# Twelve units of work between seven products: two lots of six in place of three of four

## The chip, the core and the metric

The program runs on one core of a Trainium2 chip. Its time is the device time of one execution in microseconds. The kernel is a chain of an attention layer and two feed-forward layers, all in float32 accuracy; TensorE (PE in the rows) does the products, VectorE (DVE), ScalarE (ACT) and GpSimd (POOL) read results out and prepare operands, and SyncE (SP) issues the transfers.

## The reference

Shapes: q, k, v are 4 x 8 x 576 x 64 (batch, heads, sequence, head size); w_in of both layers is 512 x 2048 and w_out 2048 x 512; there are 2304 tokens.

```python
scores = np.where(mask, scale * q @ kT + bias, -1e9)      # window of 128 keys, slopes per head
attn = softmax(scores) @ v                                # 2304 x 512 after the heads are joined
h = attn @ moe_w_in;  r = np.maximum(h, 0);  x = (r * r) @ moe_w_out
h = x @ moe2_w_in;    sp = np.log1p(np.exp(h));  out = (h * np.tanh(sp)) @ moe2_w_out
```

The change lies in the last line, the second layer: a product with w_in, the function h * tanh(softplus(h)), called Mish, and a second product with w_out.

## The kernel before, in words

Every float32 operand is split into a high part and a low part, and a product is the sum of three matmuls: high by high, high by low, low by high. Attention and the first layer fill the first 500 us.

The second layer takes its 2304 tokens in three superblocks of 768 and walks through 24 groups, eight per superblock (the loop `for g in range(24)`). In a group the first product is made by Strassen's scheme (in Winograd's form): seven products of half blocks instead of eight. Each is a call of `product` (matmuls in line 1174): six pairs of a weight load and a matmul, of which the rows show six matmuls of 128 x 384, into one bank of PSUM. In groups 1 to 8 the products use two banks in turn (`turns["p"] % 2`), so product n+2 may start when the result of product n has been read out.

Seven products give four results, c11, c22, c12 and c21, which the read-outs put together: product 1 is copied by ScalarE (line 1731); VectorE reads the others with a sum or a difference (lines 1734, 1738, 1742, 1745 and 1747, 1751, 1756 for products 2 to 7). Behind each of the four results ScalarE applies Mish twice (`mish`, lines 1197 and 1198), and VectorE makes the low part g from the two (`mish_low`, line 1203), which `done()` calls behind the next read-out.

In the first superblock (groups 0 to 7) the second product is a plain one. Its work for a group is 12 units (`o_chunk`, lines 1217 to 1219: three matmuls of 128 x 512 into one of six accumulators, acc 0 to 5), and they are run in the group that follows, groups 1 to 8, in the gaps between its seven products. The list `share` says how many units are run behind each product. Units 1 to 6 work on c11 and c22 of the group before, units 7 to 12 on c12 and c21.

The rest of the loop body is done behind the units of the same gap, in groups 1 to 7: `ring2_load` brings and splits the rows of w_out (casts in line 1155 on ScalarE, low parts in line 1159 on VectorE), `t_prepare` makes sums of them for the later superblocks, which use Strassen's scheme in the second product too (two differences on VectorE, line 1254, behind product 4 and two behind product 6; two casts in line 1259 on ScalarE behind product 7), and `t_lows` makes their low parts (line 1265, behind product 2 of the next group). In groups 4 to 7 `run_jobs` also prepares the input of the next superblock in steps, one behind each of products 2, 4, 5, 6 and 7: subtractions on GpSimd (line 1091), casts on ScalarE (line 1096) and low parts on VectorE (line 1100). Every engine works through its instructions in the order in which the program issues them.

Of the kernel before, what the change touches and what calls it, by code (L numbers as in the profile page):

```python
# [33 lines left out]
def two_layers(  # L34
# [541 lines left out]
    def m_out(l, j, fc, part):  # L576
        n = size[j]
        if fc == 0 and part == 0:
            per = 512 // n
            t = [  # L580
                ps_o.tile([P, 512], F32, tag=f"o{e}", name=f"o{l}_{j}_{e}")
                for e in range(KC // per)
            ]
            ops_[l, j] = [t[e // per][:, e % per * n :] for e in range(KC)] if per > 1 else t
        wh, wl = whl[l, ways[j][fc]]
        g = gs[l, j, fc]
        first, last = fc == 0, fc == FC - 1


        per, r = 512 // n, slice(0, n)  # L590
        for e in range(KC):
            o, ws = ops_[l, j][e][:, r], slice(DM + e * P, DM + (e + 1) * P)
            if part == 0:
                start = first and e % per == 0
                nc.tensor.matmul(o, wh[:, ws], g[:, 0, r], start=start, stop=False)  # L595
                nc.tensor.matmul(o, wl[:, ws], g[:, 0, r], start=False, stop=False)  # L596
            else:
                stop = last and e % per == per - 1
                nc.tensor.matmul(o, wh[:, ws], g[:, 1, r], start=False, stop=stop)  # L599
        if part == 1:  # L600
            gs.pop((l, j, fc))
# [50 lines left out]
    def relu2_b(a):  # L652
        g, gg, n = a
        nc.vector.tensor_tensor(  # L654
            g[:, 1, 0:n], gg[:, 0:n], g[:, 0, 0:n].bitcast(F32), op=ALU.subtract
        )
# [487 lines left out]
    def ring2_load(g, k):  # L1144
        if k == 0:
            for e in range(2):
                t = raw2[e] = ap["c"].tile([P, DM], F32R, tag="c", name=f"v{g}_{e}", bufs=4)
                nc.sync.dma_start(out=t.bitcast(F32), in_=w2d[2 * g + e])
        elif k == 3:
            for e in range(2):  # L1150
                n = 2 * (g % 2) + e
                ring2[g, e] = [
                    xp.tile([P, 512], F32R, tag=f"x{hl}{n}", name=f"v{hl}{g}_{e}") for hl in "hl"
                ]
                nc.scalar.copy(ring2[g, e][0], raw2[e].bitcast(F32))
        elif k == 4:
            for e in range(2):
                hi, lo = ring2[g, e]
                nc.vector.tensor_tensor(
                    lo, raw2[e].bitcast(F32), hi.bitcast(F32), op=ALU.subtract  # L1160
                )
# [39 lines left out]
    def mish_low(a):  # L1201
        t, u = a
        nc.vector.tensor_tensor(t[:, 1, :], u, t[:, 0, :].bitcast(F32), op=ALU.subtract)
# [3 lines left out]
    def o_chunk(s, g, t, f, h, c):  # L1207

        first, last = g % 8 == 0 and f == h, g % 8 == 7 and f != h
        k = 3 * h + c  # L1210
        if g % 8 == 0 and (s, k) not in acc:
            acc[s, k] = (ps_o if k < 4 else ps_b).tile(
                [P, 512], F32, tag=f"o{k}", name=f"acc{s}_{k}"
            )
        o, (wh, wl) = acc[s, k], ring2[g, f]
        hi, lo = (t[:, z, c * P : (c + 1) * P] for z in range(2))
        nc.tensor.matmul(o, hi, wh, start=first, stop=False)  # L1217
        nc.tensor.matmul(o, hi, wl, start=False, stop=False)  # L1218
        nc.tensor.matmul(o, lo, wh, start=False, stop=last)  # L1219
# [64 lines left out]
    def block_tile(s, b, pair_):  # L1284
        k = 4 * pair_ + b
        name = f"a{s}_{b}_{pair_}"
        if k < 14:
            return ap["x"].tile([P, 2, TH], F32, tag=f"x{k}", name=name)
        if k == 14:
            return ap["x"].tile([P, 2, TH], F32, tag="g1", name=name)  # L1290
        return gp.tile([P, 2, 512], F32, tag="g", name=name, bufs=2)[:, :, 0:TH]
# [385 lines left out]
    for g in range(24):  # L1677
        s, m = divmod(g, 8)
        units_ = []
        if g == 0:  # L1680
            relu2_b(pend)
            ring2_load(0, 4)
            units_ = [lambda: m_out(*prev, 0), lambda: m_out(*prev, 1)]
            share = [1, 1, 0, 0, 0, 0, 0]
        elif g < 9:
            for k, (f, h) in enumerate(((0, 0), (1, 1), (0, 1), (1, 0))):
                for c in (2, 0, 1) if k == 3 else range(3):
                    t = todo[k]
                    units_.append(
                        lambda t=t, f=f, h=h, c=c, s=(g - 1) // 8, g=g - 1: o_chunk(s, g, t, f, h, c)  # L1690
                    )
            share = [0, 4, 0, 4, 0, 4, 0]
        else:
            share = [0] * 7
        todo, lows = [], []

        def done():
            while lows:
                mish_low(lows.pop(0))

        def made_of(u, name):
            if s:
                a, e = blocks2[s, BLK[name[1:3]], m // 2], m % 2
                nc.scalar.activation(a[:, e, :], u, AF.Mish)  # L1704
                return
            a = mish(u, name)
            todo.append(a[0])
            lows.append(a)

        if s and m % 2 == 0:  # L1710
            for b in range(4):
                blocks2[s, b, m // 2] = block_tile(s, b, m // 2)
        sub, add = ALU.subtract, ALU.add
        tt = nc.vector.tensor_tensor
        for k, (a, x) in enumerate(
            (
                ("a11", "b11"),
                ("a12", "b21"),
                ("s2", "t2"),
                ("s3", "t3"),  # L1720
                ("s1", "t1"),
                ("s4", "b22"),
                ("a22", "t4"),
            )
        ):
            if g == 16:
                run_jobs(1)
            ps = product(g, s, k, a, x)
            if k == 0:
                p1 = u_tile(f"p1_{g}")  # L1730
                nc.scalar.copy(p1, ps)
            elif k == 1:
                u = u_tile(f"c11_{g}")
                tt(u, ps, p1, op=add)
                made_of(u, f"g11_{g}")
            elif k == 2:
                u2 = u_tile(f"u2_{g}")
                tt(u2, ps, p1, op=add)
                done()
            elif k == 3:  # L1740
                u3 = u_tile(f"u3_{g}")
                tt(u3, ps, u2, op=add)
            elif k == 4:
                u = u_tile(f"c22_{g}")
                tt(u, ps, u3, op=add)  # L1745
                u4 = u_tile(f"u4_{g}")
                tt(u4, ps, u2, op=add)
                made_of(u, f"g22_{g}")
            elif k == 5:
                u = u_tile(f"c12_{g}")  # L1750
                tt(u, ps, u4, op=add)
                done()
                made_of(u, f"g12_{g}")
            else:
                u = u_tile(f"c21_{g}")
                tt(u, u3, ps, op=sub)
                done()
                made_of(u, f"g21_{g}")
            for _ in range(share[k]):
                units_.pop(0)()  # L1760
            if g == 0 and k == 2:
                m_evac(0, NB - 1)
            if (g, k) in ((8, 6), (9, 1), (9, 3)):
                o_evac(0, {6: 2, 1: 0, 3: 1}[k])
            if 4 <= g < 8 and k in (1, 3, 4, 5, 6):
                run_jobs(1)
            if 0 < g < 9 and k == 1:
                t_lows(g - 1)
            if 0 < g < 8:
                ring2_load(g, k)  # L1770
                t_prepare(g, k)
            if g == 16 and k == 3:
                flush()
            if s and m and k == 0:
                sums3(s, m - 1)
            if s and m in (3, 4, 5, 6) and k in (1, 4):
                t_load(s, 2 * (m - 3) + (k == 4))
            if s and m == 7 and 2 <= k < 6:
                low2(s, k - 2)
            if s and m == 7 and 1 <= k < 5:  # L1780
                high2(s, k - 1)
            if g + 2 < 24 and g not in (14, 15) and k in (1, 4, 5, 6):
                ring1_load((g + 2) % 8, g + 2, ("ra", "rc", "rd", "rb")[max(k - 3, 0)])
            if 0 < g < 10 and k == (5 if g == 9 else 2):
                store_later()
        done()
        if g == 0:
            jobs += x_prepare(1)
        if s and m == 7:
            products2(s)  # L1790
# [85 lines left out]
```

## Time and profile before

| | us |
|---|---|
| time, median of 3 runs | 865.79 (865.5 to 866.45) |
| the profiled execution | 866.81 |
| its span, first to last instruction | 864.9 |
| TensorE busy (matmuls) | 857.0 (99%) |
| VectorE busy | 624.5 (72%) |
| ScalarE busy | 498.8 (58%) |
| GpSimd busy | 249.4 (29%) |

Groups 1 to 8, with which the change deals, lie between 509 and 634 us. A matmul's rows overlap, since the engine starts one before the one ahead has left it; the distance between two starts is what a matmul costs, and a row of x6 is a whole product. VectorE's rows overlap a little in the same way. "Idle before, releaser" in brackets is the time in which the engine stood still before the row, and what ended it.

### The profile page before, as it was taken

How to read it: one execution, taken by the hardware profiler on the slowest of the kernel's cores; microseconds unless marked ns; L12 is line 12 of the kernel's file. 1: busy time of each engine (PE TensorE's matmuls, PEld its weight loads, DVE VectorE, ACT ScalarE, POOL GpSimd, SP SyncE). 2: the span in 40 equal slices, each digit the busy share in tenths (PEclk: the TensorE clock that was granted, in tenths of full speed). 3: DMA queues.
4: the chain of work that ended last, by engine and by line, in shares of the span. 5: the costliest groups of instructions: out<-in, count | busy, mean ns of one | idle time of the engine just before them, and what ended most of it. 6: DMA issues, size and time to landing. Idle time of an engine off the chain costs nothing.

```text
span 864.9 us, 14890 instructions
## 1 busy us (share of the span) xinstructions
PE 857.0 (99%) x4794; PEld 752.7 (87%) x4794; DVE 624.5 (72%) x1414; ACT 498.8 (58%) x1179; POOL 249.4 (29%) x301
## 2 busy tenths in 40 slices
PE   8999999999999999999999999999999999999998
PEld 5688889998888888888888899999899999999887
DVE  5899998646596979876767456578645688755984
ACT  6888887876565656555555464545433547234641
POOL 4411213745665646643002100022024200144000
PEclk9999999999999999999999999999999999999999
DMA  8366694853765758765666978798879598988574
GB/s 285 111 219 208 197 319 140 276 185 96 269 225 207 226 152 289 249 212 168 211 214 223 364 243 290 260 313 291 268 237 366 188 306 282 316 278 281 190 266 152
DMA packets 109757, 206.98 MB, mean 239 GB/s; under 512 B 13808, under 2 KB 49008, under 8 KB 109680
## 3 DMA queue, kind: packets, MB, share of 16 engines
q1 hardware_dynamic: 109680, 206.03, 71.4%
q8 instruction: 39, 0.64, 0.3%
q14 instruction: 38, 0.31, 0.1%
HBM read 154.60 MB, written 51.38 MB: 238 GB/s over the span
## 4 chain that ended last, share of the span: by engine, by line
PE 96%; DMA 1%; DVE 1%; SPq 0%; POOL 0%; issue 0%; ACT 0%; POOLq 0%
PE h L567 23%; PE p L1174 20%; PE m L1406 11%; PE o L595 8%; PE o L596 8%; PE o L599 8%; PE o L505 3%; PE acc L1218 3%; PE acc L1219 3%; PE acc L1217 3%; PE m L1395 2%; PE pt L429 1%; PE sc L334 1%; PE sc L333 1%; PE o L526 1%; DMA wraw<-in_w 1%
## 5 line engine op out<-in xcount | busy, mean ns | idle before, releaser
L595 PE MATMUL o<-g,wh 128*128 128x512 f32 (+1 forms) x320 | 118.5, 377 | 0.0
L596 PE MATMUL o<-g,wl 128*128 128x512 f32 (+1 forms) x320 | 115.9, 369 | 0.0
L635 ACT ACTIVATE r<-h 128x512 f32<-128x512 f32 (+1 forms) x80 | 44.3, 553 | 94.3 <-PE h L567 86.0
L567 PE MATMUL h<-xh,wh 128*128 128x512 f32 (+1 forms) x320 | 81.5, 376 | 0.0
L654 DVE TENSOR_TENSOR g<-gg,g 128x512 fp32r<-128x512 f32 (+1 forms) x80 | 59.9, 749 | 29.8 <-ACT g L649 21.7
L567 PE MATMUL h<-xl,wh 128*128 128x512 f32 (+1 forms) x320 | 79.0, 369 | 0.0
L599 PE MATMUL o<-g,wh 128*128 128x512 f32 (+1 forms) x320 | 79.0, 369 | 0.0
L1704 ACT ACTIVATE a<-c 128x384 f32<-128x384 f32 x64 | 33.7, 526 | 78.5 <-DVE c L1745 41.8
L567 PE MATMUL h<-xh,wl 128*128 128x512 f32 (+1 forms) x320 | 78.8, 368 | 0.0
L465 POOL TENSOR_SCALAR_AFFINE_SELECT pT<-p 128x128 f32<-128x128 f32 (+2 forms) x80 | 52.6, 679 | 90.7 <-ACT p L453 90.5
L595 PEld LDWEIGHTS o<-g,wh 128*128 128x128 f32 x320 | 60.3, 189 | 9.8 <-issue 0.5
L596 PEld LDWEIGHTS o<-g,wl 128*128 128x128 f32 x320 | 60.4, 189 | 9.3
L1406 PE MATMUL m<-tt,hi 128*128 128x512 f32 x280 | 66.0, 390 | 0.0
L567 PEld LDWEIGHTS h<-xl,wh 128*128 128x128 f32 x320 | 56.9, 189 | 10.4
L599 PEld LDWEIGHTS o<-g,wh 128*128 128x128 f32 x320 | 56.8, 189 | 10.3
L567 PEld LDWEIGHTS h<-xh,wl 128*128 128x128 f32 x320 | 56.9, 189 | 10.1
L261 POOL TENSOR_TENSOR ulo<-uraw,uhi 128x256 fp32r<-128x256 f32 (+1 forms) x44 | 43.6, 991 | 70.8 <-ACT uhi L258 51.0
L387 ACT ACTIVATE p<-p,st 128x128 f32<-128x128 f32 (+1 forms) x144 | 59.0, 412 | 8.4 <-DVE st L372 8.3
L1406 PEld LDWEIGHTS m<-tt,hi 128*128 128x128 f32 x280 | 51.9, 188 | 10.2
L567 PEld LDWEIGHTS h<-xh,wh 128*128 128x128 f32 x320 | 54.3, 189 | 7.3 <-ACT xh L544 0.3
L1304 POOL TENSOR_TENSOR s<-a,a 128x384 f32<-128x384 f32 x14 | 14.2, 1012 | 155.9 <-ACT a L1704 155.9
L1174 PE MATMUL p<-x_t,rc 128*128 128x384 f32 x288 | 58.2, 336 | 0.0
(162 smaller groups left out, 2045.8 us busy)
## 6 DMA issues: line engine op xcount, KB each, us to landing
wraw<-in_w SPq DMA_DIRECT2D x64, 512.0 KB, 4.5
tt<-t2d SPq DMA_DIRECT2D x112, 256.0 KB, 4.6
ra<-w1d SPq DMA_DIRECT2D x24, 512.0 KB, 5.4
rc<-w1d SPq DMA_DIRECT2D x24, 512.0 KB, 4.5
rd<-w1d SPq DMA_DIRECT2D x24, 512.0 KB, 5.1
uraw<-in_qkT SPq DMA_DIRECT2D x24, 320.0 KB, 4.6
uraw<-in_qkT SPq DMA_DIRECT2D x24, 256.0 KB, 5.1
wh<-wsd SPq DMA_DIRECT2D x12, 512.0 KB, 6.4
```

Of the source, the lines that this page charges most:

```text
L261: sub(u.lo[:, 0 : u.nk], u.raw[:, 256:n], u.hi[:, 256:n].bitcast(F32), op=ALU.subtract)
L387: nc.scalar.activation(probs(i, s), probs(i, s), AF.Exp, bias=u.st[:, s : s + 1], scale=-1.0, accum_out=u.st[:, sums + s : sums + 1 + s],)
L465: nc.gpsimd.affine_select(out=u.pT[:, 0:heads, k : 2 * n : 2, :][:, :, a:], in_=p[:, 0:heads, a:n], pattern=[[0, heads * (n - a)], [0, P / ...
L567: nc.tensor.matmul(ph[:, 0:n], w[:, c * P : (c + 1) * P], xs[j, c][k][:, 0:n], start=t == 0, stop=t == len(terms) - 1,)
L595: nc.tensor.matmul(o, wh[:, ws], g[:, 0, r], start=start, stop=False)
L596: nc.tensor.matmul(o, wl[:, ws], g[:, 0, r], start=False, stop=False)
L599: nc.tensor.matmul(o, wh[:, ws], g[:, 1, r], start=False, stop=stop)
L635: nc.scalar.activation(r[:, 0:n], ph[:, 0:n], AF.Relu)
L654: nc.vector.tensor_tensor(g[:, 1, 0:n], gg[:, 0:n], g[:, 0, 0:n].bitcast(F32), op=ALU.subtract)
L1174: nc.tensor.matmul(ps, w[:, z, c * P : (c + 1) * P], t[c], start=n == 0, stop=n == 5)
L1406: nc.tensor.matmul(o[c][:, r], a, ts2[s, q][:, r], start=start, stop=stop)
L1704: nc.scalar.activation(a[:, e, :], u, AF.Mish)
```

## The change

One list of numbers is another. The seven entries are the gaps behind products 1 to 7 of a group, for groups 1 to 8.

```diff
-            share = [0, 4, 0, 4, 0, 4, 0]
+            share = [0, 6, 0, 0, 6, 0, 0]
```

Before, four units stood behind each of products 2, 4 and 6. Now six stand behind product 2 and six behind product 5. The order of VectorE's, ScalarE's, GpSimd's and SyncE's instructions is the same in both kernels; only TensorE's changes.

The first place is TensorE in group 1, from the last unit of the first lot on (`acc` are units, `p` are products 3, 4 and 5, three rows each):

```order
+L1219 MATMUL acc_5_6181<-vh_1_6013,g_0_6100 128x512
+L1174 MATMUL p_1_6189<-x_t_5759,rc_5968 128x384 x2
+L1174 MATMUL p_1_6189<-x_t_5760,rc_5968 128x384 x2
+L1174 MATMUL p_1_6189<-x_t_5759,rc_5968 128x384 x2
+L1174 MATMUL p_1_6207<-x_t_5763,rd_5970 128x384 x2
+L1174 MATMUL p_1_6207<-x_t_5764,rd_5970 128x384 x2
+L1174 MATMUL p_1_6207<-x_t_5763,rd_5970 128x384 x2
+L1174 MATMUL p_1_6226<-x_t_5767,rc_5968 128x384 x2
+L1174 MATMUL p_1_6226<-x_t_5768,rc_5968 128x384 x2
+L1174 MATMUL p_1_6226<-x_t_5767,rc_5968 128x384 x2
 L1217 MATMUL acc_3_6173<-vh_0_6010,g_0_6115 128x512
```

Product 5, which stood behind a lot, now follows product 4 directly, and the second lot follows it.

The second place is TensorE at the end of the same group, behind the last unit (products 6 and 7):

```order
 L1219 MATMUL acc_1_6165<-vh_1_6013,g_0_6130 128x512
+L1174 MATMUL p_1_6262<-x_b_5815,rd_5970 128x384 x2
+L1174 MATMUL p_1_6262<-x_b_5816,rd_5970 128x384 x2
+L1174 MATMUL p_1_6262<-x_b_5815,rd_5970 128x384 x2
 L1174 MATMUL p_1_6279<-x_t_5819,rb_5966 128x384 x2
 L1174 MATMUL p_1_6279<-x_t_5820,rb_5966 128x384 x2
```

Product 6, which stood ahead of the last lot, now stands behind it, so that products 6 and 7 and then 1 and 2 of the next group follow each other.

The third place is VectorE in group 4, from the read-out of product 6 to that of product 7, in the changed kernel:

```order
L1751 TENSOR_TENSOR c_4_6759<-p_4_6752,u_4_6718 128x384
L1203 TENSOR_TENSOR g_4_6720<-c_4_6716,g_4_6720 128x384
L1100 TENSOR_TENSOR x_b_6746<-xb_1_0_6656,x_b_6745 128x384
L1254 TENSOR_TENSOR t_4_0_6705<-v_1_6624,t_4_0_6705 128x256
L1254 TENSOR_TENSOR t_4_1_6706<-t_4_0_6705,v_1_6624 128x256
L1756 TENSOR_TENSOR c_4_6781<-u_4_6693,p_4_6774 128x384
```

Here nothing moved: before the change the same six stand in the same order, with other buffer numbers. In groups 1 to 3 the row of line 1100 isn't there, in group 8 only the first and the last are.

## Rows read from the trace of the kernel before

**Rows 1.** Page, part 4: the chain that ended last, share by engine.

```profile
PE 96%; DMA 1%; DVE 1%; SPq 0%; POOL 0%; issue 0%; ACT 0%; POOLq 0%
```

**Rows 2.** Windows of groups 3, 4: us, busy by engine, PEclk, DMA share, GB/s.

```profile
540.46:556.10 15.64, 15.64 (x80) 14.11 (x79) 9.51 (x19) 6.73 (x13) 0.00 (x0) 1.00 0.82 268
556.10:571.74 15.64, 15.64 (x80) 14.11 (x79) 11.50 (x20) 7.45 (x15) 4.42 (x4) 1.00 0.91 311
```

**Rows 3.** Waits of weight loads, 500 to 865: total us, times, longest.

```profile
PEld p L1174 <- ACT p L1731: 0.3, 1, 0.3
```

**Rows 4.** Timeline of PE, group 3: start us, us, engine, line, operation.

```profile
540.46 2.24 PE L1174 MATMUL p<-x_b,ra 128*128 128x384 f32 x12
...
542.54 0.39 PE L1217 MATMUL acc<-vh,g 128*128 128x512 f32 x1
...
545.30 1.23 PE L1174 MATMUL p<-x_t,rc 128*128 128x384 f32 x6
546.36 1.20 PE L1174 MATMUL p<-x_t,rd 128*128 128x384 f32 x6
...
555.03 1.23 PE L1174 MATMUL p<-x_t,rb 128*128 128x384 f32 x6
556.10 2.24 PE L1174 MATMUL p<-x_b,ra 128*128 128x384 f32 x12
```

**Rows 5.** Timeline of DVE and ACT, group 3 (1756 belongs to product 7 of group 2).

```profile
540.65 0.55 DVE L1756 TENSOR_TENSOR c<-u,p 128x384 f32<-128x384 f32 x1 [0.92 <-PE p L1174]
...
542.36 0.56 DVE L1203 TENSOR_TENSOR g<-c,g 128x384 fp32r<-128x384 f32 x1 [0.68 <-ACT c L1198]
...
543.26 0.47 ACT L1731 COPY p<-p 128x384 f32<-128x384 f32 x1
...
553.57 0.55 DVE L1751 TENSOR_TENSOR c<-p,u 128x384 f32<-128x384 f32 x1
...
554.04 0.55 DVE L1203 TENSOR_TENSOR g<-c,g 128x384 fp32r<-128x384 f32 x1
...
554.50 0.42 DVE L1254 TENSOR_TENSOR t<-v,t 128x256 f32<-128x256 f32 x1
...
554.96 0.42 DVE L1254 TENSOR_TENSOR t<-t,v 128x256 f32<-128x256 f32 x1
```

**Rows 6.** Timeline of DVE, groups 4 and 5: spacings of lines 1100 and 1254.

```profile
570.14 0.55 DVE L1100 TENSOR_TENSOR x_b<-xb,x_b 128x384 fp32r<-128x384 f32 x1
570.61 0.42 DVE L1254 TENSOR_TENSOR t<-v,t 128x256 f32<-128x256 f32 x1
...
579.82 0.42 DVE L1254 TENSOR_TENSOR t<-v 128x256 f32<-128x256 f32 x1
580.16 0.42 DVE L1254 TENSOR_TENSOR t<-v,v 128x256 f32<-128x256 f32 x1
...
587.17 0.43 DVE L1254 TENSOR_TENSOR t<-t,v 128x256 f32<-128x256 f32 x1
587.58 0.55 DVE L1756 TENSOR_TENSOR c<-u,p 128x384 f32<-128x384 f32 x1
```

**Rows 7.** Timeline, start of group 9: products 1 and 2, ScalarE's copy, product 4.

```profile
634.30 2.25 PE L1174 MATMUL p<-x_b,ra 128*128 128x384 f32 x12
...
635.98 0.48 ACT L1731 COPY p<-p 128x384 f32<-128x384 f32 x1
...
637.67 1.20 PE L1174 MATMUL p<-x_t,rd 128*128 128x384 f32 x6
```

**Rows 8.** Timeline of POOL and DVE, group 4.

```profile
562.59 1.01 POOL L1091 TENSOR_TENSOR t<-xb,xb 128x384 f32<-128x384 f32 x1 [82.27 <-DMA xb<-x1d]
562.68 1.34 DVE L1203 TENSOR_TENSOR g<-c,g 128x384 fp32r<-128x384 f32 x1
...
566.92 1.01 POOL L1091 TENSOR_TENSOR t<-t,xb 128x384 f32<-128x384 f32 x1
567.07 0.56 DVE L1745 TENSOR_TENSOR c<-p,u 128x384 f32<-128x384 f32 x1 [1.10 <-PE p L1174]
```

## The prediction

> **What bounds the kernel now.** The chain of waits comes first: 96% of it is TensorE [rows 1], so the question is only whether TensorE gets other work or other waits. Second, the table of windows, cut at the starts of the groups that the change touches: a group lasts 15.64 us and TensorE is busy for 15.64 of them, at a granted clock of 1.00, its full level; group 4, in which GpSimd works too, is as long as group 3 [rows 2]. There is nothing to win here but seams. Third, the list of waits of the weight loads (they run ahead of the matmuls and so meet a semaphore first): from 500 us to the end it holds one line, 0.3 us in total [rows 3]. TensorE waits for nobody behind this stage either, so what is lost here arrives at the end in full.
>
> Fourth, TensorE's own timeline in group 3 [rows 4]. I call the products of a group 1 to 7, and X the start of product 7. Products 1 and 2 take 2.08 us together (540.46 to 542.54), so 1.04 each; four units of the second product take 2.76 (542.54 to 545.30), so six take 4.14. The product behind a lot is 0.03 longer than the one behind a product (1.23 against 1.20; 555.03 to 556.10 is 1.07). Now these products alternate between two banks: product n+2 can begin only when the result of product n has been read out. Lots of units lie between most such pairs and give the reader time. The run 7, 1, 2 is the longest without a lot now.
>
> Fifth, VectorE in the same group [rows 5]. It reads product 7 (line 1756) from 540.65, 0.19 after product 1 has started, for 0.55, until 541.20; product 2 starts at 541.50. So this hand-off has 0.30 us of air, and VectorE is free when it is wanted. What it does behind product 6 is the important part: the read-out of product 6 (line 1751, 553.57), then the low part of c22 (line 1203, 554.04), then two differences for the t matrices (line 1254, 554.50 and 554.96). Before the change all this lies under four units and product 7.
>
> **The change part by part.** *The lots.* Nothing is added or taken away: 12 units per group in 8 groups before and after, and each row on VectorE, ScalarE, GpSimd and in the DMA queue keeps its place in its own queue; only TensorE's rows move. TensorE's sequence from one lot to the next was 2, 2 and 3 products long; it is now 3 (products 3, 4, 5) and 4 (6, 7, 1, 2). One lot less per group is one seam less: 8 x 0.03, so 0.2 us gained at most, and no less than nothing.
>
> *The lots' inputs and what their reading frees.* Every unit comes as early as before or earlier, and its inputs come from the group before: the last of them, the low part of c21, is done at 542.36 + 0.56 = 542.92, 1.7 us behind read-out 7 [rows 5], and the second lot, which reads it, stands behind product 5. The tiles that the units read come free earlier. No wait from here: 0.
>
> *The run 3, 4, 5.* Product 5 now needs the read-out of product 3 with only product 4 in between. That is the distance that 7, 1, 2 has now: 0.19 + 0.55 behind the next product's start, 0.30 of air [rows 4, 5]. VectorE has had a lot of 4.14 us before it to work off its queue. 0, but with little air.
>
> *The run 6, 7, 1, 2.* Three hand-offs. Product 1 needs read-out 6: VectorE is idle ahead of it, so 0.19 + 0.55 again, 0. Product 2 needs read-out 7, and that stands in VectorE's queue behind the four instructions that follow product 6. Earlier these were under four units; now product 7 ends while they run. From the rows: read-out 6 starts at X + 0.19; low of c22 0.47 later, the first difference 0.46 after that, the second 0.46 (it needs the first), and read-out 7 follows a difference by 0.34 (579.82 to 580.16) to 0.41 (587.17 to 587.58) [rows 5, 6]. So it starts at X + 1.92 to 1.99 and ends 0.55 later, at X + 2.47 to 2.54. Product 2 is due at X + 2.08. It is late by 0.39 to 0.46.
>
> What lateness costs beyond itself: in the only stall of the later trace ScalarE's copy ends at 635.98 + 0.48 = 636.46, product 3 was due at 634.30 + 2.08 = 636.38, and the product behind it starts at 637.67 and not at 637.42 [rows 7]. Late by 0.08, lost 0.25: 0.17 on top, since the weight load has to go ahead and the pipeline to fill. I take the same here: 0.56 to 0.63, middle 0.60.
>
> In groups 4 to 7 one more instruction stands in that queue, the low part of a tile for the next superblock (line 1100), 0.47 long (570.14 to 570.61) [rows 6]. There the loss is 1.03 to 1.10, middle 1.07. Both differences are made in groups 1 to 7, so it is the passages 1|2, 2|3, 3|4 at 0.60 and 4|5, 5|6, 6|7, 7|8 at 1.07: 1.80 + 4.28 = 6.08 us. In group 8 nothing stands between the two read-outs: 0.
>
> *Behind the stall.* Does it breed another? ScalarE's copy of product 1 ends 2.53 us after read-out 7 (541.20 to 543.73) [rows 5], so at about X + 5.0; product 3, which wants that bank, is due at X + 2.65 + 1.04 + 4.14 = X + 7.8. In groups 4 to 7 one more cast runs on ScalarE, the size of the copy, and the air is still over 2 us. The queue for the DMA waits for products and read-outs too, but loads for a group are issued two groups ahead, so half a microsecond is hidden by 15. Nothing.
>
> *GpSimd.* Its four subtractions in group 4 run from 562.59 to 567.93, and there the low part of a g tile took 1.34 us instead of 0.55 [rows 5, 8]. They end 11.8 us behind the start of the group (556.10); the queue behind product 6 starts 15.2 us or more behind it. I count 0. That a VectorE instruction stretches so has its rule in the Trainium skill (SBUF — State Buffer, Who interferes with whom): one with two inputs in SBUF waits out a GpSimd instruction that reads SBUF, one with at most one doesn't. The trace agrees with both halves: a read-out from PSUM that starts at 567.07, while the last subtraction runs, takes 0.56 [rows 8].
>
> *Sum.* 6.08 - 0.2 = 5.9 us. The profiled execution took 866.81 us, 1.0 more than the median of 865.79; the loss is the same for both: 872.7 there, 871.7 as a median. The ends of this case: without the 0.17 for the restart 3 x 0.43 + 4 x 0.90 - 0.2 = 4.7; with the long ends throughout 6.3 - 0. So 870.5 to 872.1.
>
> **The rivals.** *A: VectorE is in time, not slower.* The two differences need loads that are long there, so they could be done while the second lot of units runs, where VectorE has idle time; then read-out 7 is not late and one seam per group is saved: 865.6. It decides at a queue of 1.2 us from read-out 6 to read-out 7: 0.19 + 1.2 + 0.55 + 0.17 is about 2.08. Against it: the order of VectorE's rows puts both differences behind read-out 6, and in the trace each engine keeps its order; what the rows show is 1.73 or more. For it: only that the spacing of these instructions could shrink. 6%.
>
> *B: the tight hand-offs fail as well.* Products 3 to 5 and 6 to 1 have 0.30 of air, and 0.17 of it is wanted for an undisturbed start. If the air is gone, by a tenth or two of delay on VectorE, 16 hand-offs lose some 0.15 each: 2.4 more, 874.1. Against it: today's 7 to 2 has the same air and loses nothing in seven passages. 10%.
>
> *C: GpSimd's subtractions get into the queue behind product 6* in groups 4 and 6: at least one instruction stretched in each, 2 x (1.34 - 0.55) = 1.6 more, 873.3. It takes loads that land 3.4 us later than now. 3%. The page named above gives the mechanism; the price is the rows'.
>
> *D: half as much.* If the restart costs nothing on top (7 x 0.17 = 1.2 less) and all spacings in the queue but the first are 0.34, as where a difference follows one that it doesn't need (2 x 0.12 x 7 = 1.7 less), 6.08 - 2.9 - 0.2 = 3.0 are left: 868.8. Against it: 554.50 to 554.96 has the spacing of the dependent pair. 9%.
>
> **How the numbers follow.** The forecast as worked out has 72%, A 6%, B 10%, C 3%, D 9%. The likeliest is 871.7. The range takes in D's upper end, B and C: 869.0 to 874.5; outside stay A, and the ends of B and D. About 0.2%, 1.7 us, is what a measurement of this kernel can tell from no change. Faster by more would need more than all seams of the stage give (24 x 0.03 = 0.7 us): 1%. Within it: A and the smallest of D, 7%. Slower: 92%.
>
> **What would show it.** In the changed kernel's list of waits of the weight loads a line for products (1174) behind VectorE's line 1756 has to appear, seven times, six to seven microseconds in all. Cut at the starts of product 1, group 1 stays at 15.6 us, groups 2 to 4 go to about 16.2, groups 5 to 8 to about 16.7. Read-out 7 has to start without idle time right behind the second difference, 1.7 us behind read-out 6, or 2.2 in groups 4 to 7. The stage from group 9 on keeps its length. I am wrong if product 2 follows product 1 without a gap (A), if gaps stand ahead of product 5 or 1 (B), or if line 1254 or 1100 is stretched behind product 6 (C).

## The result and the profile after

The changed kernel takes 870.73 us against 865.64 before, a ratio of 1.0055 with a 95% interval of 1.0044 to 1.0067: by the ratio about 4.8 us slower (3.8 to 5.8). In a second comparison (e1_again, below) it is 871.31 against 865.59, 1.0062 (1.0048 to 1.0076), so 5.4 us (4.2 to 6.6). The forecast was 871.7, 5.9 us slower.

One of the six executions of the changed kernel, the one profiled first, ran TensorE at about half its pace from beginning to end (1716.93 us): it counts in the median of 870.73 but not in the ratio. The rows here are those of the same program in e1_again, which took 872.17 us in the profiled execution, 5.36 more than the profiled execution before.

The page of the changed kernel, part 4, the chain by engine (before: [rows 1]):

```profile
PE 94%; DVE 3%; DMA 1%; issue 1%; SPq 0%; POOL 0%; ACT 0%; POOLq 0%
```

The list of waits of the weight loads from 500 us on (us in total, times, longest; before: [rows 3]):

```profile
PEld p L1174 <- DVE c L1756: 6.2, 7, 1.1
PEld p L1174 <- ACT p L1731: 0.3, 1, 0.3
```

The first line is new: seven times a product waits for VectorE's read-out of product 7. The windows of groups 1 to 8, cut at the starts of product 1 (us, busy time by engine with the number of rows, PEclk, DMA share, GB/s; before: [rows 2]):

```profile
509.27:524.87 15.60, 15.60 (x79) 14.12 (x79) 8.87 (x18) 5.87 (x12) 0.00 (x0) 1.00 0.91 305
524.87:541.02 16.15, 15.86 (x79) 14.06 (x79) 9.41 (x20) 6.64 (x14) 0.00 (x0) 1.00 0.81 261
541.02:557.19 16.17, 15.88 (x79) 14.07 (x79) 9.42 (x20) 6.65 (x14) 0.00 (x0) 1.00 0.80 260
557.19:573.33 16.14, 15.85 (x79) 14.05 (x79) 11.35 (x20) 7.04 (x15) 4.39 (x4) 1.00 0.93 310
573.33:589.96 16.63, 15.87 (x79) 14.07 (x79) 11.76 (x25) 8.68 (x19) 0.00 (x0) 1.00 0.80 254
589.96:606.60 16.64, 15.88 (x80) 14.08 (x79) 12.21 (x22) 7.45 (x16) 4.40 (x4) 1.00 0.89 299
606.60:623.23 16.63, 15.87 (x79) 14.07 (x79) 11.76 (x25) 8.68 (x19) 0.00 (x0) 1.00 0.81 253
623.23:639.86 16.63, 15.87 (x79) 14.07 (x79) 7.83 (x16) 4.96 (x11) 0.00 (x0) 1.00 0.71 221
```

The table has the three steps of the forecast: group 1 isn't longer than before, groups 2 to 4 are at 16.15, groups 5 to 8 at 16.63. Together they last 639.86 - 509.27 = 130.59 us. Before the change they last from 509.14 (the row below) to 634.30 [rows 7], 125.16 us: 15.68 for group 1 and 15.64 for each of the others. So the stage is 5.4 us longer, and that is the whole loss: the profiled executions differ by 5.36. The granted clock is 1.00 throughout. The row of the kernel before with which group 1 starts:

```profile
509.14 2.27 PE L1174 MATMUL p<-x_b,ra 128*128 128x384 f32 x12
```

One short passage and one long one in the timeline (start us, us, engine, line, operation; before: [rows 4, 5]). First the passage from group 3 to group 4, from product 7 on:

```profile
556.15 1.20 PE L1174 MATMUL p<-x_t,rb 128*128 128x384 f32 x6
...
556.35 0.56 DVE L1751 TENSOR_TENSOR c<-p,u 128x384 f32<-128x384 f32 x1 [2.87 <-PE p L1174]
556.83 0.55 DVE L1203 TENSOR_TENSOR g<-c,g 128x384 fp32r<-128x384 f32 x1
...
557.02 1.05 PEld L1174 LDWEIGHTS p<-x_b,ra 128*128 128x128 f32 x6
557.19 1.21 PE L1174 MATMUL p<-x_b,ra 128*128 128x384 f32 x6
557.29 0.42 DVE L1254 TENSOR_TENSOR t<-v,t 128x256 f32<-128x256 f32 x1
...
557.74 0.42 DVE L1254 TENSOR_TENSOR t<-t,v 128x256 f32<-128x256 f32 x1
...
558.09 0.55 DVE L1756 TENSOR_TENSOR c<-u,p 128x384 f32<-128x384 f32 x1
...
558.68 1.00 PEld L1174 LDWEIGHTS p<-x_b,ra 128*128 128x128 f32 x6 [0.61 <-DVE c L1756]
558.69 1.31 PE L1174 MATMUL p<-x_b,ra 128*128 128x384 f32 x6 [0.29 <-DVE c L1756]
...
559.84 0.39 PE L1217 MATMUL acc<-vh,g 128*128 128x512 f32 x1
```

Product 7's row ends at 557.35, and VectorE is then in the first of its two differences. Read-out 7 starts at 558.09 without idle time, ends at 558.64, and product 2 starts 0.05 later. It was due at 557.19 + 1.04 = 558.23. Undisturbed, a product's first weight load (PEld) starts 0.17 ahead of its first matmul (557.02 and 557.19). Behind the wait both start together, and product 2 takes 1.15 to the next start (559.84) and not 1.04.

Then the passage from group 4 to group 5, which has the instruction of line 1100 in the queue as well:

```profile
572.29 1.20 PE L1174 MATMUL p<-x_t,rb 128*128 128x384 f32 x6
...
572.49 0.56 DVE L1751 TENSOR_TENSOR c<-p,u 128x384 f32<-128x384 f32 x1 [0.95 <-PE p L1174]
572.97 0.55 DVE L1203 TENSOR_TENSOR g<-c,g 128x384 fp32r<-128x384 f32 x1
...
573.33 1.21 PE L1174 MATMUL p<-x_b,ra 128*128 128x384 f32 x6
573.43 0.55 DVE L1100 TENSOR_TENSOR x_b<-xb,x_b 128x384 fp32r<-128x384 f32 x1
...
574.70 0.55 DVE L1756 TENSOR_TENSOR c<-u,p 128x384 f32<-128x384 f32 x1
...
575.30 1.33 PE L1174 MATMUL p<-x_b,ra 128*128 128x384 f32 x6 [0.76 <-DVE c L1756]
```

Read-out 7 comes 2.21 us behind read-out 6 here, and 1.74 in the short passage. "0.29" and "0.76" in brackets are less than the time lost, because a matmul's row lasts longer than the distance to the next.

### The profile page after: what moved, and what is told of

Read it like the earlier page. It is cut to its first block, busy times and chain, and to the rows that moved or that the text cites. A ratio compares the mean times of both kernels' runs of the same rounds, so it can differ in the third digit from the quotient of the medians.

```text
span 1715.2 us, 14885 instructions
## 1 busy us (share of the span) xinstructions
PE 1710.2 (100%) x4794; PEld 1257.2 (73%) x4794; DVE 606.0 (35%) x1414; ACT 502.9 (29%) x1179; POOL 230.2 (13%) x301
## 4 chain that ended last, share of the span: by engine, by line
PE 100%; POOL 0%; DVE 0%; issue 0%; POOLq 0%
PE h L567 24%; PE p L1174 21%; PE m L1406 11%; PE o L595 8%; PE o L596 8%; PE o L599 8%; PE o L505 3%; PE acc L1218 3%; PE acc L1219 3%; PE acc L1217 3%; PE m L1395 2%; PE pt L429 2%; PE sc L333 1%; PE sc L334 1%; PE o L526 1%; PE sc L310 1%
## 5 line engine op out<-in xcount | busy, mean ns | idle before, releaser
L595 PE MATMUL o<-g,wh 128*128 128x512 f32 (+1 forms) x320 | 203.7, 638 | 0.0
L596 PE MATMUL o<-g,wl 128*128 128x512 f32 (+1 forms) x320 | 199.6, 626 | 0.0
L567 PE MATMUL h<-xh,wh 128*128 128x512 f32 (+1 forms) x320 | 156.5, 642 | 0.0
L599 PE MATMUL o<-g,wh 128*128 128x512 f32 (+1 forms) x320 | 151.9, 627 | 0.0
L567 PE MATMUL h<-xl,wh 128*128 128x512 f32 (+1 forms) x320 | 150.8, 627 | 0.0
L567 PE MATMUL h<-xh,wl 128*128 128x512 f32 (+1 forms) x320 | 150.7, 632 | 0.0
L1406 PE MATMUL m<-tt,hi 128*128 128x512 f32 x280 | 133.4, 674 | 0.0
L595 PEld LDWEIGHTS o<-g,wh 128*128 128x128 f32 x320 | 97.2, 304 | 41.7 <-issue 37.8
L599 PEld LDWEIGHTS o<-g,wh 128*128 128x128 f32 x320 | 92.3, 308 | 43.7 <-issue 37.0
L1174 PE MATMUL p<-x_b,ra 128*128 128x384 f32 x288 | 105.7, 558 | 0.0
L1174 PEld LDWEIGHTS p<-x_t,rc 128*128 128x128 f32 x288 | 87.2, 304 | 15.9 <-issue 11.0
L1174 PEld LDWEIGHTS p<-x_b,ra 128*128 128x128 f32 x288 | 86.9, 305 | 14.9 <-issue 10.0
```

Source lines behind the costliest of these rows:

```text
L567: nc.tensor.matmul(ph[:, 0:n], w[:, c * P : (c + 1) * P], xs[j, c][k][:, 0:n], start=t == 0, stop=t == len(terms) - 1,)
L1174: nc.tensor.matmul(ps, w[:, z, c * P : (c + 1) * P], t[c], start=n == 0, stop=n == 5)
L1406: nc.tensor.matmul(o[c][:, r], a, ts2[s, q][:, r], start=start, stop=stop)
```

## The experiments

Two theories stood against each other. The queue theory says that the time is lost only because read-out 7 stands behind other work in VectorE's queue when products 6, 7, 1 and 2 follow each other. The order theory says that the new order of products and units costs by itself, through the tight hand-offs and the seams. Times of the kernel before in the same comparisons: 865.59 us for e1 to e4, 865.03 for e5 to e8.

**e1_again**, the changed kernel.

> The changed kernel once more, for an undisturbed trace. Queue theory (read-out 7 stands on VectorE behind the low part of c22, the two t differences and, in groups 4 to 7, the low part of line 1100): 870.6 us; seven waits of product 2 for line 1756, about 0.5 to 0.65 us each in groups 2 to 4 and 0.9 to 1.1 in groups 5 to 8; group 1 stays at 15.6. Rival, order theory (the new order of products and units costs by itself, at the tight hand-offs from product 3 to 5 and 6 to 1 and at the seams): the same time, but gaps of 0.1 to 0.3 us ahead of products 5 and 1 in all eight groups, group 1 and group 9 among them.

871.31 us, and the rows above: waits of product 2 in groups 2 to 8, none of products 5 and 1, none in group 1.

**e2_t_early**: the second pair of differences is issued behind product 5, under the second lot.

```diff
-                t_prepare(g, k)
+                t_prepare(g, {4: 5, 5: 4}.get(k, k))
```

> The changed kernel with the second pair of t differences issued behind product 5 instead of product 6, so that they lie under the second lot. Queue theory: nothing is late in passages 1|2 to 3|4; in 4|5 to 7|8 read-out 7 starts at X + 0.19 + 3 x 0.47 = 1.60 and ends at 2.15, 0.07 behind the due time, 0.07 to 0.24 lost each; the time is 865.6 - 0.2 + 0.3 to 1.0 = 865.7 to 866.4. Order theory: VectorE's queue doesn't matter, 870.6 stays.

865.7 us, ratio 0.9999 (0.9990 to 1.0009). Its waits, and the windows of a group behind a short passage (3) and behind a long one (6):

```profile
PEld p L1174 <- DVE c L1756: 1.1, 4, 0.3
```

```profile
538.94:554.51 15.57, 15.57 (x79) 14.08 (x79) 9.59 (x20) 6.81 (x14) 0.00 (x0) 1.00 0.81 270
585.91:601.74 15.83, 15.83 (x79) 14.06 (x79) 11.43 (x22) 7.37 (x16) 4.35 (x4) 1.00 0.94 315
```

Of seven waits four are left, of 0.3 us, and those are the four passages in which line 1100 still stands in the queue. Two differences in another place on VectorE give the time back, with the lots where the change put them: the order theory is gone. By the rows some 0.5 us of loss is left (four passages of 15.83 - 15.57 = 0.26, less the 0.56 that e3 below shows for fewer lots), which the ratio is too wide to show. VectorE's rows in the passage from group 4 to group 5, from read-out 6 to read-out 7:

```profile
569.25 0.56 DVE L1751 TENSOR_TENSOR c<-p,u 128x384 f32<-128x384 f32 x1 [0.43 <-PE p L1174]
...
570.66 0.55 DVE L1756 TENSOR_TENSOR c<-u,p 128x384 f32<-128x384 f32 x1
```

**e3_both_early**: as e2, and the step of line 1100 goes too. The steps are one list, worked off in order, so not this step alone moves: those that stood behind products 4, 5 and 6 now stand behind 3, 4 and 5.

```diff
-            if 4 <= g < 8 and k in (1, 3, 4, 5, 6):
+            if 4 <= g < 8 and k in (1, 2, 3, 4, 6):
```

> As e2, and in groups 4 to 7 the step for the next superblock that stood behind product 6 is issued behind product 3, so that only the low part of c22 stands between read-outs 6 and 7. Queue theory: no passage is late, one seam per group is saved, 865.4 against 865.6 before the change, which can't be told apart. Order theory: 870.6.

865.0 us, ratio 0.9991 (0.9982 to 1.0000). No wait for VectorE is left, and its groups are shorter than those before the change. Windows of groups 2 and 6, and TensorE around the first lot of group 4:

```profile
524.05:539.62 15.57, 15.57 (x79) 14.09 (x79) 9.60 (x20) 6.71 (x14) 0.00 (x0) 1.00 0.83 271
586.35:601.92 15.57, 15.57 (x79) 14.08 (x79) 11.73 (x22) 7.52 (x16) 4.28 (x4) 1.00 0.95 320
```

```profile
557.27 0.39 PE L1217 MATMUL acc<-vh,g 128*128 128x512 f32 x1
...
561.39 1.23 PE L1174 MATMUL p<-x_t,rc 128*128 128x384 f32 x6
562.46 1.20 PE L1174 MATMUL p<-x_t,rd 128*128 128x384 f32 x6
563.50 1.20 PE L1174 MATMUL p<-x_t,rc 128*128 128x384 f32 x6
```

15.57 against 15.64 [rows 2]: one lot less saves 0.07 per group, 0.5 in all. Products 3, 4 and 5 follow each other without a gap. Its groups are the shortest of all the kernels here; by its time alone it can just about not be told from the one before.

**e4_run_of_four**: the kernel before with only the run 6, 7, 1, 2.

```diff
-            share = [0, 4, 0, 4, 0, 4, 0]
+            share = [0, 4, 0, 4, 4, 0, 0]
```

> The kernel before with the last lot of four moved ahead: four units behind each of products 2, 4 and 5. The run 3, 4, 5 isn't made, the run 6, 7, 1, 2 is. Queue theory: the whole loss of the change and one seam more per group than it, 870.6 to 871.0. Order theory: one of the two new kinds of run is gone, the loss is about half, 868.

871.34 us, ratio 1.0063 (1.0049 to 1.0077). Windows of groups 3 and 6:

```profile
539.71:555.93 16.22, 15.93 (x79) 14.08 (x79) 9.51 (x20) 6.65 (x14) 0.00 (x0) 1.00 0.80 259
588.86:605.55 16.69, 15.93 (x79) 14.08 (x79) 11.52 (x22) 7.46 (x16) 4.37 (x4) 1.00 0.91 298
```

Against 15.64 this is 0.58 and 1.05 lost. The run of four alone makes the whole loss, and with three lots a group is 0.05 to 0.07 longer than in e1_again.

**e5_run_of_three**: only the run 3, 4, 5.

```diff
-            share = [0, 4, 0, 4, 0, 4, 0]
+            share = [0, 6, 0, 0, 2, 4, 0]
```

> Six units behind product 2, two behind product 5, four behind product 6: the run 3, 4, 5 is made, the run 6, 7, 1, 2 isn't (7, 1, 2 stands as before the change). Queue theory: nothing is late, three lots as before the change, 865.6. Order theory (what is left of it: the hand-off from product 3 to 5 loses by itself): some tenths in each of eight groups, 867 or more.

865.15 us, ratio 1.0001 (0.9992 to 1.0010). Windows of groups 3 and 6:

```profile
539.05:554.66 15.61, 15.61 (x80) 14.10 (x79) 9.50 (x19) 6.64 (x13) 0.00 (x0) 1.00 0.84 270
585.87:601.48 15.61, 15.61 (x80) 14.09 (x79) 11.66 (x21) 7.45 (x15) 4.28 (x4) 1.00 0.94 318
```

TensorE has no gap. The tight hand-off from product 3 to product 5 costs nothing. But with three lots a group is 15.61 and not 15.64 as expected: a lot of two costs less than a lot of four (below).

**e6_t_twice**: the pair of differences is computed twice.

```diff
-            for o, a, b in todo_:
+            for o, a, b in todo_ * (2 if k == 5 and m > 0 else 1):
```

> The changed kernel in which the second pair of t differences is computed twice, one after the other with the same values, in groups 1 to 7: two more instructions of 0.46 us between read-outs 6 and 7. Queue theory: each passage loses 0.92 more, one for one, 7 x 0.92 = 6.4, so 871.0 + 6.4 = 877.4. If product 2 waited for something else than the end of this queue, less than half of that, 871 to 874.

876.4 us, ratio 1.0130 (1.0114 to 1.0145). Windows of groups 3 and 6, and VectorE's queue behind product 6 of group 2:

```profile
540.74:557.81 17.07, 15.86 (x80) 14.06 (x79) 10.26 (x22) 6.64 (x14) 0.00 (x0) 1.00 0.78 246
592.44:609.97 17.53, 15.85 (x80) 14.04 (x79) 12.94 (x24) 7.45 (x16) 4.39 (x4) 1.00 0.88 284
```

```profile
540.84 0.42 DVE L1254 TENSOR_TENSOR t<-v,t 128x256 f32<-128x256 f32 x1
541.29 0.42 DVE L1254 TENSOR_TENSOR t<-t,v 128x256 f32<-128x256 f32 x1
541.75 0.42 DVE L1254 TENSOR_TENSOR t<-v,t 128x256 f32<-128x256 f32 x1
542.21 0.42 DVE L1254 TENSOR_TENSOR t<-t,v 128x256 f32<-128x256 f32 x1
542.55 0.55 DVE L1756 TENSOR_TENSOR c<-u,p 128x384 f32<-128x384 f32 x1
```

A group is 0.90 (17.07 - 16.17) and 0.89 (17.53 - 16.64) longer than in e1_again, and the two more instructions take 0.92 (541.29 to 542.21). The queue is paid one for one, to 0.03. The time is a microsecond under the 877.4 expected; the kernel before is 0.56 faster in this comparison than in that of e1_again, from which the expectation started.

**e7_job_early**: the differences stay, the step of line 1100 goes, with the two steps ahead of it (the edit of e3 to the steps alone).

> The changed kernel with the step for the next superblock issued behind product 3 instead of product 6 in groups 4 to 7; the t differences stay. Queue theory: passages 4|5 to 7|8 lose 0.55 like the others instead of 1.03, 1.9 less, 871.0 - 1.9 = 869.1. If groups 5 to 8 were slower for another reason (GpSimd's subtractions, the loads of the next superblock), 871.0 stays.

869.08 us, ratio 1.0048 (1.0034 to 1.0062). Windows of groups 3 and 6:

```profile
540.73:556.90 16.17, 15.87 (x80) 14.07 (x80) 9.41 (x20) 6.65 (x14) 0.00 (x0) 1.00 0.80 260
589.21:605.37 16.16, 15.87 (x80) 14.06 (x79) 11.42 (x22) 7.57 (x16) 4.68 (x4) 1.00 0.93 308
```

Group 6 falls from 16.64 to 16.16 and is then like group 3. The instruction of line 1100 in the queue made groups 5 to 8 longer than 2 to 4. GpSimd's subtractions, which belong to the steps that moved as well, ran in group 4 at nearly the same time as before the move (564.32 to 569.15 here, 563.81 to 569.12 in e1_again), and in e1_again groups 5, 7 and 8 are as long as group 6 without any, so they are not the reason.

**e8_old_lots_both_early**: the kernel before, with its three lots of four and e3's two moves.

> The kernel before with the two moves of e3 and its own three lots of four. If what e3 gains against the kernel before (0.6 us) comes from one seam less in each of eight groups, nothing changes here: groups of 15.64 us, 865.6. If it comes from the moves, 865.0.

865.02 us, ratio 0.9995 (0.9987 to 1.0004). Windows of groups 3 and 6:

```profile
539.21:554.85 15.64, 15.64 (x79) 14.11 (x79) 9.50 (x19) 6.75 (x13) 0.00 (x0) 1.00 0.84 271
586.13:601.77 15.64, 15.64 (x79) 14.11 (x79) 12.29 (x21) 7.58 (x16) 4.54 (x4) 1.00 0.94 320
```

The moves alone change no group. What e3 gains comes from its two lots.

## Why the prediction was right, point by point

**Direction and cause.** Right, and shown from both sides: take the queue behind product 6 away and the loss goes (e2, e3), lengthen it and it grows one for one (e6), make the run 6, 7, 1, 2 alone and the loss is all there (e4).

**The chain from read-out 6 to read-out 7.** Forecast 1.73 to 1.80 us, measured 1.74; with line 1100 2.20 to 2.27, measured 2.21. The spacings came from rows of the same instructions under other work of TensorE, and they held: 0.48, 0.46, 0.45 and 0.35, forecast 0.47, 0.46, 0.46 and 0.34 to 0.41.

**Lateness and restart.** Product 2 is late by 0.41 in the short passage (558.64 against 558.23; forecast 0.39 to 0.46) and by 0.88 in the long one (575.25 against 574.37). The time lost, against the undisturbed 15.57 of e3, is 16.15 - 15.57 = 0.58 and 16.63 - 15.57 = 1.06; forecast 0.60 and 1.07. The extra 0.17 for the restart, read from a single stall in another group, is there again: 0.58 - 0.41 = 0.17, 1.06 - 0.88 = 0.18. Its two parts are in the rows of the short passage: 0.05 from the end of read-out 7 to product 2, and 0.11 by which product 2 then takes longer. That the weight load goes ahead of the matmul, the reason that the forecast gave, fits these rows; that the pipeline has to fill is not shown. The loss is 3 x 0.58 + 4 x 1.06 = 5.98, forecast 6.08.

**The seams: the term that was mis-sized.** I took 0.03 for a seam, the excess of the product behind a lot, and 0.2 for the eight, and I took six units at half as much again as four, 4.14. The seam is 0.07 (15.64 - 15.57), 0.56 for the eight. I had looked at one end of a lot only. The other half lies in the lot: four units take 2.76 [rows 4], six take 4.12 (557.27 to 561.39 in e3), so the fifth and sixth take 0.68 each and the first four 0.69, some 0.04 more per lot than at the later pace. With it the sum is 5.98 - 0.56 = 5.4, which is what the trace shows (5.4 in the stage, 5.36 in the executions). Of the microsecond by which the forecast of 871.7 was high, the seams and the passages explain half. The rest is no more than the spread of the runs: the same two programs differ by 4.8 us in one comparison and by 5.4 in the other.

A seam has no fixed price either. In e5 a lot of two costs 0.04 (15.61 - 15.57): its two units take 1.39, 0.03 more than at the later pace, and the product behind it has no excess (1.04 to the next start). Why the first units of a lot are slower stays open; they differ from the products in shape and in operands, and no run separates the two.

**What I counted at nothing.** The two other new hand-offs have not lost anything (e5, and no wait of product 5 or 1 in e1_again): rival B is out. ScalarE's copy and the queue for the transfers bred no further wait. GpSimd's subtractions stretch VectorE's instructions in group 4 as before, and they stop well ahead of the queue behind product 6. Rows of the changed kernel:

```profile
565.66 1.01 POOL L1091 TENSOR_TENSOR t<-xb,xb 128x384 f32<-128x384 f32 x1 [0.83 <-DMA xb<-x1d]
565.70 1.38 DVE L1203 TENSOR_TENSOR g<-c,g 128x384 fp32r<-128x384 f32 x1
...
568.04 1.08 POOL L1091 TENSOR_TENSOR t<-t,xb 128x384 f32<-128x384 f32 x1
```

They end at 569.12, and read-out 6 starts at 572.49, again 3.4 us later (in group 6 at 602.30 and 605.75): rival C is out by the margin that was worked out. That a VectorE instruction with two inputs in SBUF waits out GpSimd's reading is the rule of the Trainium skill named in the prediction (SBUF — State Buffer, Who interferes with whom); this trace agrees again, with 1.38 us in place of 0.55.

**Rivals A and D.** VectorE was not in time, and not by half either: its rows in these passages stand in the order of the program, and read-out 7 waits behind both differences. D falls with both its parts, since the 0.17 for the restart is there and so are the spacings of 0.46. The bound of A, a queue of some 1.2 us from read-out 6 to read-out 7, was tried in passing: in e2's long passages the queue is 1.41 (569.25 to 570.66), and 0.26 is lost each time (15.83 - 15.57); in its short passages, with only the low part of c22 between the two, nothing is lost. Where between them the bound lies was not measured.

## What to carry to other kernels

When two banks are used in turn, ask of every run of products without other work between them what the reading engine has in its queue between two read-outs, and not only how long a read-out takes: the sum of those rows, with the distance of two products as its limit and 0.17 us for each restart, gave the loss of the seven passages to a tenth of a microsecond. Work that only has to be done sometime (sums, low parts, the next stage's operands) belongs behind a product that is followed by a lot of other work; a change of the lots has to move it along. Here the four units behind product 6, which looked like a seam too many, were VectorE's time to catch up.

## What the runs showed of the hardware

One thing was not expected. A lot of units between products costs at its start as well as behind its end: its first three units take 0.69 to 0.70 us, the later ones 0.68, and the product behind a lot of four or six takes 0.03 more; behind a lot of two it does not (e5).

The other was read from one stall and held in four more cases: a stall costs TensorE 0.17 to 0.18 us beyond the lateness itself, the same for 0.08 us (e2's long passages: read-out 7 ends at 571.21, product 2 was due at 571.13, lost 0.26), for 0.41 and 0.88 (the changed kernel) and for 1.32 (e6: 543.10 against 541.78, lost 17.07 - 15.57 = 1.50), with the granted clock at 1.00 in these groups.
